# First-layer expert weights loaded in 16 transfers from ScalarE's DMA queue instead of 40 from SyncE's, with three reorderings in the attention steps

## The chip, the cores and the metric

One core of a Trainium2 chip. The metric is the device time of one launch in microseconds (us); the times below are medians over runs.

## What is computed

Three layers follow each other on 2 batches of 768 tokens with 8 heads of 40 (320 features). The first is a gated linear attention, written in the reference as a recurrence over time:

```python
m_new = np.maximum(f_gate[:, :, t] + m, i_gate[:, :, t])
f_stab = np.exp(f_gate[:, :, t] + m - m_new)
i_stab = np.exp(i_gate[:, :, t] - m_new)
C = f_stab[:, :, None, None] * C + i_stab[:, :, None, None] * np.einsum('bhd,bhe->bhde', vt, kt)
n = f_stab[:, :, None] * n + i_stab[:, :, None] * kt
h_tilde = np.einsum('bhde,bhe->bhd', C, qt)
nq = np.einsum('bhd,bhd->bh', n, qt)[:, :, None]
denom = np.maximum(np.abs(nq), 1.0)
y[:, :, t] = o * h_tilde / denom          # o = sigmoid(o_gate)
```

The second is a soft mixture of 8 experts with 4 slots each: `logits = x @ phi`, a softmax over tokens gathers 32 slot inputs, each expert does `relu(s @ w1[e]) @ w2[e]` (w1 is 320 x 1024, w2 1024 x 320), and a softmax over slots spreads the results to the tokens. The third is a mixture of 4 dense experts over all 1536 tokens with weights u1 and u2 of the same sizes. All data are 32-bit floats.

## The kernel before, in words

Every engine's instructions are written out by hand in one order (`tc.manual_schedule()`); the framework only adds the waits. Each DMA gets one of eight completion semaphores, dealt out in turn in the program's order over all issuing engines, and a DMA is issued only after the DMA before it on its semaphore has landed.

**Attention** goes over NT = 12 tiles of 128 tokens, i = 0 to 11, the two batches in turn. The loop `for i in range(2, NT - 1)` interleaves stages of several tiles: `stage_S(i)` multiplies q and k on TensorE, `stage_W` masks and scales on VectorE, `stage_E(i + 1)` makes the next tile's decay matrix (TensorE, then two exponentials on ScalarE), `stage_P1(i - 1)` multiplies with v, `stage_K(i + 2)` transposes k on TensorE (`stage_KT`, L313) and copies it out on ScalarE (`stage_KC`, L318), `q_pad`, `qT_mm` and `qT_copy` do so for q, `stage_B` takes the absolute value of the denominator on ScalarE (L394), which `stage_N` then uses on VectorE (L399), `stage_X` and `stage_XC` transpose a finished tile. The gates of tiles are made by `gates1a`, `gates1b`, `gates_hi` and `gates2`, for the last piece (chunks 4 and 5) in steps 3 to 6. All transposes and the decay matrices share three PSUM banks with the tag "t".

**Loads.** Everything comes through SyncE's queue (SP), in program order: per step one k tile (`load_k`, L198), one v tile (`load_v`, L205), one or two o_gate tiles (`load_o`, L220), in some steps q (`load_q`), each 160 KB in runs of 160 bytes, and between them w1 in 40 pieces of 256 KB (`load_w1`, L88: one of five rows per partition each). The table NW says how many pieces stand in each step; the last is issued after the attention. k, v and q rotate through few buffers, so their loads wait for the engines that read the buffer before.

**First mixture.** When the attention's memory is free, w2 is loaded in 16 transfers of 640 KB (`load_w2`, L96), while TensorE does logits, gather and the w1 products (L1119), then the w2 products (L1155). Behind w2 come u1 and u2 of the first dense expert.

**Second mixture.** From about 120 us TensorE runs without a break (L1268, L1284).

Of the kernel before, what the change touches and what calls it, by code (L numbers as in the profile page):

```python
# [8 lines left out]
F32 = mybir.dt.float32  # L9
# [5 lines left out]
NEG = -1.0e30  # L15
NBIG = 11
NW3 = 5
NW = (0, 0, 4, 4, 4, 4, 4, 4, 4, 4, 3, 2)
WN = (2, 4, 2, 4)


# [1 line left out]
def tile_mlstm_soft_moe_domain_moe(  # L23
# [57 lines left out]
    u1s = {}  # L81
    u2s = {}

    def load_w1(n, r):
        half, j = divmod(n, 4)
        if r == 0:
            w1s[half, j] = slot([128, 5, FH], f"w1_{n}")
        nc.sync.dma_start(  # L88
            out=w1s[half, j][:, r],
            in_=w1[2 * j:2 * j + 2, :, half * FH:half * FH + FH].rearrange("e (p r) f -> r (e p) f", r=5)[r],  # L90
        )

    def load_w2(e, u, get):
        if u == 0:
            w2s[e] = get([128, 2, R2, DM], f"w2_{e}")
        nc.sync.dma_start(out=w2s[e][:, u], in_=w2[e, u * FH:(u + 1) * FH].rearrange("(p r) d -> p r d", r=R2))  # L96
# [10 lines left out]
            u2s[e] = get([128, FT, DM], f"u2_{e}")  # L107
        nc.sync.dma_start(out=u2s[e][:, r0:r1], in_=u2[e, r0 * 128:r1 * 128].rearrange("(r p) d -> p r d", p=128))

    wq = [("a", n, r) for n in range(8) for r in range(5)] + [("b", e, u) for e in (0, 2, 4, 6) for u in range(2)]  # L110
    wq += [("b", e, u) for e0 in (1, 5) for u in range(2) for e in (e0, e0 + 2)]

    def load_w(n=1, get=None):
        for _ in range(n):
            if wq:
                kind, x, u = wq.pop(0)
                if kind == "a":
                    load_w1(x, u)
                else:
                    load_w2(x, u, get or slot)  # L120

    with tc.manual_schedule():
        mctx = ExitStack()
# [9 lines left out]
        with ExitStack() as actx:  # L133
# [258 lines left out]
            def stage_B(i):  # L392
                dn = wp.tile([128, H], F32, tag="dn", name="dn")
                nc.scalar.activation(out=dn, in_=hs[i][0][:, :, D], func=AF.Abs, scale=2.0)  # L394
                dns[i] = dn
# [56 lines left out]
                pXs[i] = pt  # L452

            def stage_XC(i):
                xT = tp.tile([128, 3, 128], F32, tag="xT", bufs=4, name="xT")
                nc.scalar.activation(out=xT, in_=pXs.pop(i)[:, 0:3], func=AF.Copy)
                xTs[i] = xT

# [19 lines left out]
                lts[i0] = (lt, et)  # L478
                return lambda: nc.scalar.activation(out=lt, in_=pl[:, 0:128], func=AF.Copy)

            def stage_M(i0, get=tt_):
                lt, et = lts.pop(i0)
                pl = get()
                nc.tensor.transpose(pl[:, 0:128], et, ident)
                dE = tp.tile([128, 128], F32, tag="dE", bufs=2, name="dE")
                nc.scalar.activation(out=dE, in_=pl[:, 0:128], func=AF.Copy)
                dEs[i0] = dE
                plg[i0] = pl
                ltk[i0] = lt

            plg = {}
            ltk = {}

            def copy_lg(i0):
                nc.tensor.transpose(plg[i0][:, 128:256], ltk.pop(i0), ident)
                nc.vector.tensor_copy(lg[:, i0:i0 + 4, :], plg.pop(i0)[:, 128:256].rearrange("p (j n) -> p j n", n=NS))

            def stage_Q(i0, get=tt_):
# [194 lines left out]
            def gates_hi(c0, c1):  # L693
                nc.scalar.activation(out=hiX[:, c0 * L:c1 * L].bitcast(F32R), in_=X[:, c0 * L:c1 * L], func=AF.Copy)
# [85 lines left out]
            stage_O(1)  # L780
            load_k(4)
            load_os()
            load_w(2)
            load_q(5)
            stage_Wk(2)
            stage_T2(1)
# [2 lines left out]
            for i in range(2, NT - 1):  # L789
                c = bc(i)[1]  # L790
                last = i == NT - 2
                stage_S(i)
                if i + 3 < NT:
                    load_k(i + 3)
                if i in (4, 5):
                    load_q(i + 2)
                load_w(1)
                load_os(2 if i in (5, 6) else 1)
                if i + 2 < NT:
                    load_v(i + 2)  # L800
                load_w(NW[i] - 1)
                if i == 3:
                    nc.sync.dma_start(out=phi_sb[:, 0:2, :], in_=phi[0:256].rearrange("(k p) n -> p k n", p=128))
                    nc.sync.dma_start(out=phi_sb[0:64, 2, :], in_=phi[256:320])
                stage_W(i, 0)
                stage_E(i + 1)
                stage_P2(i)
                if i in (3, 4, 7, 8):
                    q_pad({3: 4, 4: 5, 7: 6, 8: 7}[i], 0, 2, A_)
                stage_W(i, 1)  # L810
                if i == 2:
                    gates1b(2, 4, 0, 0)
                stage_U(i)
                stage_P1(i - 1)
                if i > 2:
                    stage_T2(i)
                stage_mask(i + 1)
                if i == 2:
                    stage_V(1)
                    stage_K(3)  # L820
                    stage_V1(1)
                    gates1b(2, 4, 0, 1)
                    stage_T2(i)
                    qT_mm(3, 0)
                    qT_copy(3, 0)
                    gates_hi(2, 4)
                    gates1b(2, 4, 1)
                    gates2(2, 4, (A_, V_, G_, G_, A_))
                if i == 6:
                    gates1b(4, NC, 1)  # L830
                stage_V(i)
                stage_T1(i - 1)
                stage_B(i - 1)
                if last:
                    break
                if i in (3, 6):
                    tokT(*((2, 4) if i == 3 else (4, NC)))
                    tokC(*((2, 4) if i == 3 else (4, NC)))
                if i == 6:
                    gates2(4, NC, (A_, V_))  # L840
                if i == 8:
                    stage_R0(stage_Q(0))
                if i == 9:
                    c_sum(0, 4)
                    emit_c4(0)
                if i == 7:
                    stage_M(0)
                    copy_lg(0)
# [24 lines left out]
                if i == 2:
                    pt = tr().rearrange("p a b -> p (a b)")
                    gate_rows(1, 4, NC, pt, 0)
                    gate_rows(0, 4, NC, pt, 2 * L)
                    gates_in(4, NC, pt[:, 0:2 * L], pt[:, 2 * L:4 * L])
                if i in (3, 4, 5):
                    gates1a(4, NC, Fg[:, 4 * L:S], (i - 3,))
                if i == 5:  # L880
                    gates1b(4, NC, 0, 0)
                    gates1b(4, NC, 0, 1)
                    gates_hi(4, NC)
                if i == 6:
                    gates2(4, NC, (None, None, G_, A_, G_))
# [124 lines left out]
        with mctx:  # L1010
# [54 lines left out]
            stage_M(8, tt_)  # L1065
# [313 lines left out]
```

## Time and profile before

| | |
|---|---|
| time, median of 3 runs | 322.2 us (321.8 to 323.55) |
| the profiled execution's own time | 323.63 us |
| its span | 321.5 us |
| TensorE busy | 304.8 us, 95% |
| VectorE, ScalarE, GpSimd busy | 168.9 us, 117.6 us, 93.2 us |
| DMA | 43.48 MB, 65518 packets, 49808 of them under 512 bytes |
| granted clock of TensorE | 1.00 (2.4 GHz) in every slice |

A profile belongs to one execution, here one that took 323.63 us; the span is what the profiler saw of it. Its first 80 us are the attention, about 80 to 120 us the first mixture, the rest the second one. Busy shares over the whole span hide the difference between these stages, so the views used here are cut by stage.

### The profile page before, as it was taken

The numbers are of one execution on the slowest core, as the hardware profiler recorded it, in microseconds if no ns is written. First come the engines' busy times: TensorE is split into PE (matmuls) and PEld (weight loads), VectorE is DVE, ScalarE is ACT, GpSimd is POOL, SyncE is SP. The second block draws the span as 40 slices with busy tenths as digits, with TensorE's granted clock in tenths as the row PEclk, the third lists the DMA queues.
The fourth block names the chain that finished last, engine by engine and source line by source line (L and its number), as shares of the span: only waits on it lengthen the run. The fifth ranks groups of instructions, "written<-read, shape, count | busy, mean of one in ns | idle before, by whom it ended". The sixth has DMA issues, their size and how long they took to land.

```text
span 321.5 us, 6949 instructions
## 1 busy us (share of the span) xinstructions
PE 304.8 (95%) x2846; PEld 266.5 (83%) x2846; DVE 168.9 (53%) x351; ACT 117.6 (37%) x259; POOL 93.2 (29%) x148
## 2 busy tenths in 40 slices
PE   8899988888899899999999999999999999999995
PEld 7787876667553348899999998999998999999995
DVE  7997997667434144564444444444443444444411
ACT  3968747553412034432222222333332222222200
POOL 8657766543602027830004600003800000000000
PEclk9999999999999999999999999999999999999999
DMA  7999979999999998129000001380001100011111
GB/s 139 195 232 215 231 205 251 217 243 296 341 417 416 387 308 200 26 59 314 0 3 0 0 2 33 78 283 2 0 0 27 42 2 0 22 41 41 43 61 41
DMA packets 65518, 43.48 MB, mean 135 GB/s; under 512 B 49808, under 2 KB 57008, under 8 KB 65488
## 3 DMA queue, kind: packets, MB, share of 16 engines
q1 hardware_dynamic: 65392, 42.99, 47.1%
q8 instruction: 22, 0.36, 0.5%
q14 instruction: 8, 0.07, 0.1%
q10 hardware_dynamic: 96, 0.07, 0.1%
HBM read 39.50 MB, written 1.97 MB: 129 GB/s over the span
## 4 chain that ended last, share of the span: by engine, by line
PE 81%; DVE 7%; DMA 6%; issue 1%; ACT 1%; SPq 1%; POOL 1%; ACTq 0%; DVEq 0%; POOLq 0%
PE po L1284 53%; PE pa L1268 7%; DMA w<-in_moe_w_dram 3%; DMA kvb<-in_k_dram 3%; PE pss L346 3%; PE po L1155 2%; PE pg L1224 2%; PE ph L1119 1%; PE p L370 1%; DVE w L352 1%; PE p L362 1%; PE pt L451 1%; PE pt L270 1%; PE pt L296 1%; PE p L544 1%
## 5 line engine op out<-in xcount | busy, mean ns | idle before, releaser
L1284 PE MATMUL po<-uh,hh 128*128 128x320 f32 x768 | 170.3, 309 | 0.6 <-ACT hh L1273 0.6
L1284 PEld LDWEIGHTS po<-uh,hh 128*128 128x128 f32 x768 | 131.7, 188 | 5.8 <-issue 1.8
L1284 PE MATMUL po<-ul,hh 128*128 128x320 f32 x384 | 118.2, 309 | 0.0
L1274 DVE SCALAR_TENSOR_TENSOR hh<-pa,hh 128x512 fp32r<-128x512 f32 x96 | 65.7, 691 | 95.5 <-ACT hh L1273 95.5
L1273 ACT ACTIVATE hh<-pa 128x512 fp32r<-128x512 f32 x96 | 56.7, 599 | 121.7 <-PE pa L1268 120.5
L1284 PEld LDWEIGHTS po<-ul,hh 128*128 128x128 f32 x384 | 72.0, 188 | 0.0
L1209 POOL TENSOR_SCALAR uh<-u 128x640 fp32r<-128x640 f32 x16 | 11.6, 728 | 93.2 <-PE po L1284 73.5
L1268 PE MATMUL pa<-cS,gs 128*128 128x512 f32 x96 | 36.9, 397 | 0.2 <-ACT gs L1262 0.2
L1211 POOL TENSOR_TENSOR ul<-u,uh 128x640 fp32r<-128x640 f32 x16 | 25.1, 1570 | 1.3
L1292 DVE SCALAR_TENSOR_TENSOR acc<-po,pr,acc 128x320 f32<-128x320 f32 x36 | 19.5, 543 | 10.6 <-PE po L1284 10.6
L1268 PEld LDWEIGHTS pa<-cS,gs 128*128 128x128 f32 x96 | 17.9, 188 | 1.2 <-issue 0.4
L352 DVE TENSOR_TENSOR w<-w,pss 128x512 f32<-128x512 f32 x24 | 15.3, 679 | 4.4 <-PE pss L346 3.4
L305 POOL TENSOR_SCALAR_AFFINE_SELECT w<-w 128x512 f32<-128x512 f32 x24 | 15.5, 668 | 6.9 <-ACT w L299 6.9
L346 PE MATMUL pss<-qT,kT 64*128 64x128 f32 x192 | 14.1, 286 | 0.0
L299 ACT ACTIVATE w<-pt 128x512 f32<-128x512 f32 x24 | 13.0, 596 | 2.4 <-PE pt L296 2.3
L346 PEld LDWEIGHTS pss<-qT,kT 64*128 64x128 f32 x192 | 11.8, 187 | 1.8 <-issue 0.7
L1155 PE MATMUL po<-w,hT 128*32 128x320 f32 x128 | 10.6, 434 | 1.3 <-DMA w<-in_moe_w_dram 1.3
L370 PE MATMUL p<-kvb,w 128*64 128x64 f32 x320 | 11.0, 222 | 0.0
L443 POOL TENSOR_TENSOR x<-x,rd 128x320 f32<-128x320 f32 x11 | 8.8, 801 | 7.0 <-DVE rd L400 7.0
L370 PEld LDWEIGHTS p<-kvb,w 128*64 128x64 f32 x320 | 10.3, 138 | 0.2 <-issue 0.2
L1155 PEld LDWEIGHTS po<-w,hT 128*32 128x32 f32 x128 | 4.2, 110 | 7.1 <-DMA w<-in_moe_w_dram 2.5
L313 PE MATMUL pt<-ident,kvb 128*128 128x128 f32 x40 | 6.4, 283 | 3.4 <-DMA kvb<-in_k_dram 3.3
(248 smaller groups left out, 310.5 us busy)
## 6 DMA issues: line engine op xcount, KB each, us to landing
w<-in_moe_w_dram SPq DMA_DIRECT2D x40, 256.0 KB, 4.5
w<-in_moe_w_dram SPq DMA_DIRECT2D x16, 640.0 KB, 11.4
u1a<-in_moe_w_dram SPq DMA_DIRECT2D x4, 1024.0 KB, 10.3
u<-in_moe_w_dram SPq DMA_DIRECT2D x3, 1280.0 KB, 10.1
kvb<-in_k_dram SPq DMA_DIRECT2D x12, 160.0 KB, 4.2
kvb<-in_v_dram SPq DMA_DIRECT2D x12, 160.0 KB, 4.3
x<-in_o_gate_dram SPq DMA_DIRECT2D x12, 160.0 KB, 4.6
out_dram<-acc SPq DMA_DIRECT2D x12, 160.0 KB, 1.8
```

The costliest lines, as they stand in the source:

```text
L299: nc.scalar.activation(out=w.rearrange("p g t -> p (g t)"), in_=pt, func=AF.Exp)
L305: nc.gpsimd.affine_select(out=w, in_=w, compare_op=ALU.is_ge, fill=0.0, base=0, pattern=[[0, HP], [1, L]], channel_multiplier=-1)
L346: nc.tensor.matmul(out=pss[j][:, g, :], lhsT=kT[i][64 * j:64 * j + 64, g, :], rhs=q_of(i)[64 * j:64 * j + 64, g, :], start=True, stop=True)
L352: nc.vector.tensor_tensor(out=w, in0=w, in1=pS.pop((i, j)), op=ALU.mult)
L370: nc.tensor.matmul(out=p1[64 * x:64 * x + 64, h, :], lhsT=W[i, h % 2][:, h // 2, 64 * x:64 * x + 64], rhs=vb(i)[:, h, :], start=True, stop ...
L1155: nc.tensor.matmul(out=pos[hf][32 * j:32 * j + 32, 0:DM], lhsT=hT[:, r, 32 * j:32 * j + 32], rhs=w2s[2 * j + hf][:, r // R2, r % R2, :], s ...
L1211: nc.gpsimd.tensor_tensor(out=lo[:, r0:r0 + 2], in0=raw[:, r0:r0 + 2], in1=hi[:, r0:r0 + 2].bitcast(F32), op=ALU.subtract)
L1268: nc.tensor.matmul(out=pa, lhsT=GS[e][0][:, ft * 128:(ft + 1) * 128], rhs=cS[:, tg * 512:(tg + 1) * 512], start=True, stop=True)
L1273: nc.scalar.activation(out=hi, in_=pa, func=AF.Relu)
L1274: nc.vector.scalar_tensor_tensor(out=lo, in0=pa, scalar=0.0, in1=hi.bitcast(F32), op0=ALU.max, op1=ALU.subtract)
L1284: nc.tensor.matmul(out=po[:, 0:DM], lhsT=x[:, sl], rhs=y[e][:, ft, :], start=(ft == 0 and n == 0), stop=(ft == FT - 1 and n == 2))
L1292: nc.vector.scalar_tensor_tensor(out=dst, in0=po[:, 0:DM], scalar=pr[:, i, e:e + 1], in1=dst, op0=ALU.mult, op1=ALU.add)
```

## The change

1. w1 is loaded by 16 transfers (two rows, then three rows, of each of 8 tiles: 512 and 768 KB) that ScalarE issues: one ahead of the loop, one in step 2 and two each in steps 3 to 9, behind the exponentials of `stage_E(i + 1)`. SyncE's queue keeps k, v, q, o_gate, phi, probs and, later, w2.
2. `stage_B(i - 1)` moves from before `stage_K(i + 2)` to after the q copies and `stage_X`, in ScalarE's order; in step 3 and in the tail it moves behind other copies.
3. The last gate piece: its first two accumulations are done one and two steps sooner, `gates1b(4, NC, 1)` in step 5 instead of 6, and `gates2` in one place, ahead of the transposes, with five engines named (A, V, G, A, G).
4. The xT tiles get five buffers instead of four, and `stage_M` transposes the logits together with their exponentials, except for the last group.

```diff
-NW = (0, 0, 4, 4, 4, 4, 4, 4, 4, 4, 3, 2)
+NW = (1, 1, 2, 2, 2, 2, 2, 2, 2, 0)
...
-    def load_w1(n, r):
+    def load_w1(n, r0, r1):
         half, j = divmod(n, 4)
-        if r == 0:
+        if r0 == 0:
             w1s[half, j] = slot([128, 5, FH], f"w1_{n}")
-        nc.sync.dma_start(
-            out=w1s[half, j][:, r],
-            in_=w1[2 * j:2 * j + 2, :, half * FH:half * FH + FH].rearrange("e (p r) f -> r (e p) f", r=5)[r],
+        nc.scalar.dma_start(
+            out=w1s[half, j][:, r0:r1],
+            in_=w1[2 * j:2 * j + 2, :, half * FH:half * FH + FH].rearrange("e (p r) f -> (e p) r f", r=5)[:, r0:r1],
         )
+
+    w1q = [(n, r0, r1) for n in range(8) for r0, r1 in ((0, 2), (2, 5))]
+
+    def act_w(k=1):
+        for _ in range(k):
+            if w1q:
+                load_w1(*w1q.pop(0))
...
             load_os()
-            load_w(2)
+            act_w(NW[0])
             load_q(5)
...
-                load_w(1)
                 load_os(2 if i in (5, 6) else 1)
                 if i + 2 < NT:
                     load_v(i + 2)
-                load_w(NW[i] - 1)
...
                 stage_E(i + 1)
+                act_w(NW[i - 1])
                 stage_P2(i)
...
                 if i == 6:
-                    gates1b(4, NC, 1)
+                    gates2(4, NC, (A_, V_, G_, A_, G_))
                 stage_V(i)
                 stage_T1(i - 1)
-                stage_B(i - 1)
...
                 if i > 2:
                     stage_X(i - 2)
+                if i != 3:
+                    stage_B(i - 1)
                 if i == 3:
                     stage_XC(1)
+                    stage_B(2)
...
-                if i in (3, 4, 5):
-                    gates1a(4, NC, Fg[:, 4 * L:S], (i - 3,))
+                if i == 3:
+                    gates1a(4, NC, Fg[:, 4 * L:S], (0,))
+                    gates1b(4, NC, 0, 0)
+                if i == 4:
+                    gates1a(4, NC, Fg[:, 4 * L:S], (1, 2))
                 if i == 5:
-                    gates1b(4, NC, 0, 0)
                     gates1b(4, NC, 0, 1)
                     gates_hi(4, NC)
+                    gates1b(4, NC, 1)
...
-            load_w(9, slot3)
+            load_w(8, slot3)
```

ScalarE's order in step 2, with the semaphores that each instruction waits for (w are the decay tiles of `stage_E(3)`, gt the result of `gates_hi`). Before:

```order
L394 ACTIVATE dn<-t_339 128x8 [waits DVE_49]
L327 ACTIVATE x_1_98<-x_1_98 128x320 [waits DMAHW7_49]
L299 ACTIVATE w<-pt 128x512 [waits PE_49] x2
L318 ACTIVATE kT<-pt 128x512 [waits PE_49]
L284 ACTIVATE qT<-pt 128x512 [waits PE_49]
L694 ACTIVATE gt_95<-gt_95 128x256 [waits DVE_49]
```

and now:

```order
L398 ACTIVATE dn<-t_339 128x8 [waits DVE_49]
L331 ACTIVATE x_1_98<-x_1_98 128x320 [waits DMAHW7_49]
L88 DMA w_0_379<-in_moe_w_dram 128x2x512 [waits DMAHW7_49]
L303 ACTIVATE w<-pt 128x512 [waits PE_49] x2
L88 DMA w_0_379<-in_moe_w_dram 128x3x512 [waits DMAHW0_49]
L322 ACTIVATE kT<-pt 128x512 [waits PE_49]
L288 ACTIVATE qT<-pt 128x512 [waits PE_49]
L702 ACTIVATE gt_95<-gt_95 128x256 [waits DVE_49]
```

Two DMA issues came between; the first waits for the o_gate load that holds DMAHW7 before it, the second for the v load on DMAHW0 (the last rows but one of the next block).

SyncE's queue around the same place (x_1 is an o_gate tile, kvb a k or v tile). Before:

```order
L220 DMA x_0_97<-in_o_gate_dram 128x8x40 [waits DMAHW4_49]
L88 DMA w_0_379<-in_moe_w_dram 128x512 [waits DMAHW5_49]
L88 DMA w_0_379<-in_moe_w_dram 128x512 [waits DMAHW6_49]
L193 DMA qb<-in_q_dram 128x8x80 [waits DMAHW7_49]
L198 DMA kvb_87<-in_k_dram 128x8x40 [waits DMAHW0_49]
L88 DMA w_0_379<-in_moe_w_dram 128x512 [waits DMAHW1_49]
L220 DMA x_1_98<-in_o_gate_dram 128x8x40 [waits DMAHW2_49]
```

and now:

```order
L224 DMA x_0_97<-in_o_gate_dram 128x8x40 [waits DMAHW4_49]
L197 DMA qb<-in_q_dram 128x8x80 [waits DMAHW5_49]
L202 DMA kvb_87<-in_k_dram 128x8x40 [waits DMAHW6_49]
L224 DMA x_1_98<-in_o_gate_dram 128x8x40 [waits DMAHW7_49]
L209 DMA kvb_87<-in_v_dram 128x8x40 [waits DMAHW0_49]
L202 DMA kvb_85<-in_k_dram 128x8x40 [waits DMAHW1_49,PE_49,Pool_49]
```

The three w1 pieces ahead of that o_gate load are gone, and no w1 piece stands between the later k, v and o_gate loads either.

ScalarE's order in step 4 (qx is `q_pad`, dn `stage_B`). Before:

```order
L299 ACTIVATE w<-pt 128x512 [waits PE_49] x2
L250 ACTIVATE qx<-qb 128x16x40 [waits DMAHW7_49]
L394 ACTIVATE dn<-t_577 128x8 [waits DVE_49]
L318 ACTIVATE kT<-pt 128x512 [waits PE_49]
L284 ACTIVATE qT<-pt 128x2x2x128 [waits PE_49] x2
```

and now:

```order
L303 ACTIVATE w<-pt 128x512 [waits PE_49] x2
L88 DMA w_2_664<-in_moe_w_dram 128x2x512 [waits DMAHW7_49]
L88 DMA w_2_664<-in_moe_w_dram 128x3x512 [waits DMAHW0_49]
L254 ACTIVATE qx<-qb 128x16x40 [waits DMAHW5_49]
L322 ACTIVATE kT<-pt 128x512 [waits PE_49]
L288 ACTIVATE qT<-pt 128x2x2x128 [waits PE_49] x2
L398 ACTIVATE dn<-t_571 128x8 [waits DVE_49]
```

The wait for VectorE went behind the k and q copies, and two DMA issues came ahead of them.

## Rows read from the trace of the kernel before

**Rows 1.** Busy time by stretch: start:end, length, busy us per engine, clock, DMA share, GB/s.

```profile
30.00:40.00 10.00, 10.00 (x167) 8.60 (x169) 8.10 (x20) 8.46 (x21) 6.19 (x10) 1.00 0.95 219
40.00:50.00 10.00, 8.68 (x165) 7.16 (x162) 9.64 (x21) 4.73 (x14) 7.47 (x11) 1.00 0.82 200
50.00:60.00 10.00, 8.75 (x163) 7.28 (x159) 6.11 (x16) 7.95 (x20) 4.80 (x8) 1.00 0.99 241
60.00:70.00 10.00, 7.21 (x130) 5.86 (x126) 6.98 (x19) 4.29 (x11) 5.35 (x9) 1.00 0.99 246
70.00:80.00 10.00, 9.28 (x198) 7.91 (x196) 7.03 (x19) 4.05 (x11) 3.75 (x7) 1.00 0.95 274
80.00:108.00 28.00, 25.25 (x242) 12.97 (x244) 11.21 (x35) 6.24 (x19) 7.39 (x20) 1.00 1.03 394
...
130.00:320.00 190.00, 188.06 (x1267) 180.02 (x1265) 84.44 (x140) 53.55 (x91) 27.29 (x24) 1.00 0.15 47
```

**Rows 2.** The chain that ended last, in order of time: start us, us, what.

```profile
50.88 4.02 DMA kvb<-in_k_dram
...
64.73 4.77 DMA kvb<-in_k_dram
...
97.20 10.61 DMA w<-in_moe_w_dram
```

**Rows 3.** Waits of TensorE, 20 to 80 us: total us, times, longest.

```profile
PE pt L313 <- DMA kvb<-in_k_dram: 3.3, 3, 1.4
PE pt L270 <- ACT gs L676: 0.8, 1, 0.8
PE pt L296 <- POOL x L443: 0.8, 1, 0.8
```

**Rows 4.** Waits of TensorE, 100 to 112 us.

```profile
PE po L1155 <- DMA w<-in_moe_w_dram: 1.3, 2, 0.9
```

**Rows 5.** ScalarE in order of time, step 2, idle before in brackets.

```profile
18.84 0.45 ACT L327 ACTIVATE x<-x 128x320 f32<-128x320 f32 x1
...
21.54 0.60 ACT L318 ACTIVATE kT<-pt 128x512 f32<-128x512 f32 x1 [1.14 <-PE pt L313]
...
22.51 0.42 ACT L694 ACTIVATE gt<-gt 128x256 fp32r<-128x256 f32 x1
```

**Rows 6.** SyncE's queue in order of time: start us, us, issue, out and source, count.

```profile
17.14 1.09 SPq L88 DMA_DIRECT2D w<-in_moe_w_dram  x2
...
19.39 1.74 SPq L88 DMA_DIRECT2D w<-in_moe_w_dram  x1
21.17 0.44 SPq L220 DMA_DIRECT2D x<-in_o_gate_dram  x1
...
73.66 4.07 SPq L88 DMA_DIRECT2D w<-in_moe_w_dram  x8
...
80.10 1.21 SPq L88 DMA_DIRECT2D w<-in_moe_w_dram  x1
81.42 17.27 SPq L96 DMA_DIRECT2D w<-in_moe_w_dram  x16
```

**Rows 7.** DMA issues of the page: count, KB each, median us from issue to landing.

```profile
w<-in_moe_w_dram SPq DMA_DIRECT2D x40, 256.0 KB, 4.5
...
x<-in_o_gate_dram SPq DMA_DIRECT2D x12, 160.0 KB, 4.6
```

**Rows 8.** How long one issue takes on SyncE (ns min/median/max), w1 and v loads.

```profile
L88 SPq DMA_DIRECT2D w<-in_moe_w_dram x40: 365/505/3043, 17.1 to 80.1; - x40
...
L205 SPq DMA_DIRECT2D kvb<-in_v_dram x12: 434/1121/1949, 5.9 to 73.2; - x12
```

**Rows 9.** VectorE in order of time, step 3.

```profile
31.79 0.19 DVE L684 TENSOR_TENSOR gs<-kv,gs 128x32 f32<-128x32 f32 x1 [1.72 <-PE kv L682]
```

**Rows 10.** Waits of ScalarE, 20 to 80 us.

```profile
ACT dn L394 <- DVE t L386: 7.0, 7, 1.5
ACT kT L318 <- PE pt L313: 6.7, 5, 2.4
```

More of the change, by code (lines that the diff above doesn't have):

```diff
@@ L108, in load_u2 @@
         nc.sync.dma_start(out=u2s[e][:, r0:r1], in_=u2[e, r0 * 128:r1 * 128].rearrange("(r p) d -> p r d", p=128))
-    wq = [("a", n, r) for n in range(8) for r in range(5)] + [("b", e, u) for e in (0, 2, 4, 6) for u in range(2)]
-    wq += [("b", e, u) for e0 in (1, 5) for u in range(2) for e in (e0, e0 + 2)]
+    wq = [(e, u) for e in (0, 2, 4, 6) for u in range(2)]
+    wq += [(e, u) for e0 in (1, 5) for u in range(2) for e in (e0, e0 + 2)]
     def load_w(n=1, get=None):
@@ L115, in load_w @@
             if wq:
[L116 to L120, printed above, removed]
+                e, u = wq.pop(0)
+                load_w2(e, u, get or slot)
     with tc.manual_schedule():
@@ L454, in stage_XC @@
             def stage_XC(i):
-                xT = tp.tile([128, 3, 128], F32, tag="xT", bufs=4, name="xT")
+                xT = tp.tile([128, 3, 128], F32, tag="xT", bufs=5, name="xT")
                 nc.scalar.activation(out=xT, in_=pXs.pop(i)[:, 0:3], func=AF.Copy)
@@ L479, in stage_L, with stage_M @@
                 return lambda: nc.scalar.activation(out=lt, in_=pl[:, 0:128], func=AF.Copy)
-            def stage_M(i0, get=tt_):
+            def stage_M(i0, get=tt_, both=True):
                 lt, et = lts.pop(i0)
@@ L484, in stage_M @@
                 nc.tensor.transpose(pl[:, 0:128], et, ident)
+                if both:
+                    nc.tensor.transpose(pl[:, 128:256], lt, ident)
                 dE = tp.tile([128, 128], F32, tag="dE", bufs=2, name="dE")
@@ L488, in stage_M @@
                 plg[i0] = pl
-                ltk[i0] = lt
+                if not both:
+                    ltk[i0] = lt
             plg = {}
@@ L494, in copy_lg @@
             def copy_lg(i0):
-                nc.tensor.transpose(plg[i0][:, 128:256], ltk.pop(i0), ident)
+                if i0 in ltk:
+                    nc.tensor.transpose(plg[i0][:, 128:256], ltk.pop(i0), ident)
                 nc.vector.tensor_copy(lg[:, i0:i0 + 4, :], plg.pop(i0)[:, 128:256].rearrange("p (j n) -> p j n", n=NS))
@@ L838, in tile_mlstm_soft_moe_domain_moe @@
                     tokC(*((2, 4) if i == 3 else (4, NC)))
-                if i == 6:
-                    gates2(4, NC, (A_, V_))
                 if i == 8:
@@ L877, in tile_mlstm_soft_moe_domain_moe @@
                     gates_in(4, NC, pt[:, 0:2 * L], pt[:, 2 * L:4 * L])
-                if i in (3, 4, 5):
-                    gates1a(4, NC, Fg[:, 4 * L:S], (i - 3,))
+                if i == 3:
[3 more added lines that the diff above has]
+                    gates1a(4, NC, Fg[:, 4 * L:S], (1, 2))
                 if i == 5:
-                    gates1b(4, NC, 0, 0)
                     gates1b(4, NC, 0, 1)
                     gates_hi(4, NC)
+                    gates1b(4, NC, 1)
                 if i == 6:
-                    gates2(4, NC, (None, None, G_, A_, G_))
                     tokM(4, NC)
@@ L928, in tile_mlstm_soft_moe_domain_moe @@
             stage_O(iL)
+            stage_B(iL - 2)
             stage_XC(iL - 3)
-            load_w(1)
             stage_S(iL)
-            load_w(NW[iL] - 1)
             stage_G(iL - 2)
@@ L1064, in tile_mlstm_soft_moe_domain_moe @@
             warm(WN[1])
-            stage_M(8, tt_)
+            stage_M(8, tt_, False)
             for j in range(4):
```

## The prediction

> **What bounds the kernel now.** I read the busy time by stretch first, since the change touches only the first 80 us and what starts behind them. From 130 to 320 us TensorE is busy 188.06 of 190 us and the DMA share is 0.15 [rows 1]: nothing here shortens that stage, it can only start sooner or later. From 30 to 80 us two things are nearly full at once: TensorE is busy 43.9 of 50 us, and the DMA share is 0.82 to 0.99. From 80 to 108 us the DMA share is 1.03. So the early part is short of DMA time as much as of TensorE time.
>
> The chain of waits, read next, says where the shortage bites. Twice a k load stands in it for four to five microseconds, and at 97.20 us a w2 transfer for 10.61 us [rows 2]. Then the waits of TensorE: between 20 and 80 us it stood 3.3 us, in three places, for k tiles that had not landed, 0.8 us behind ScalarE's gate copy and 0.8 us at `stage_E` behind GpSimd [rows 3]; in the w2 products it stood 1.3 us for w2 [rows 4]. The reader is to see that k is late because of where it stands: SyncE's queue has w1 pieces ahead of it, and the order shows four to a step.
>
> **The change, part by part.**
>
> *k, v and o_gate without w1 ahead of them.* With no w1 in SyncE's queue, a k load goes out when its buffer is free. By the order the k tile of step i + 3 needs only readers of tile i - 3, and one ScalarE step, `q_pad`, for a q load ahead of it; that is more than a step sooner than now. The three waits, 3.3 us, should go. Bounds: 0, if the loads are as late as now, and 3.3. I take 3.3, as k was at most 1.4 us late each time.
>
> *The last gate piece.* `gates2` ahead of GpSimd's other work of step 6 lets the 0.8 us wait at `stage_E` go [rows 3]; bounds 0 and 0.8, I take 0.8. The gate accumulations themselves are moved, not removed: VectorE does them in 30 to 40 us, where it is busy 8.10 of 10 us, instead of 40 to 50 us, where it is busy 9.64 [rows 1]. Cover is there but thin; I count 0, and if VectorE has no room left in step 3 the next term grows.
>
> *ScalarE's first transfer.* This is the place that can lose. ScalarE comes to it after the tanh, at 18.84 + 0.45 = 19.3 us [rows 5]. By the order it shares its semaphore with the o_gate load of step 2, and must wait until that has landed. That load went out at 21.17 us, behind three w1 pieces of 1.09 + 1.74 = 2.83 us together [rows 6]; without them at 18.3 us. With the median 4.6 us to landing [rows 7] it lands at 22.9 us. So ScalarE stands still for 3.6 us, with the exponentials of `stage_E(3)`, the k and q copies and `gates_hi` queued behind it, then spends two issues of 0.505 us each (median of w1's on SyncE [rows 8]), 4.6 us in all. The 1.14 us in which it waited for TensorE there anyway comes off [rows 5]: `gates_hi`, at 22.51 us now, is some 3.5 us late. VectorE waits for it at once, and has 1.72 us of idle time in step 3 to make up [rows 9]. So 1.8 us stay. Upper bound 3.5, with no idle time to use; lower bound 1.0, if the 0.8 us behind ScalarE's gate copy [rows 3] goes too, because `stage_B` no longer stands ahead of it. I take 1.8: the slack of VectorE is the nearest row.
>
> *ScalarE's other transfers.* Steps 3 to 9 add 14 issues: 14 x 0.505 = 7.1 us. Moving `stage_B` behind the copies takes away the 7.0 us in which ScalarE waited for VectorE with the k copy queued behind [rows 10]. The two cancel, 0 net. Bounds: 14 x 0.365 = 5.1 us and 14 x 1.121 = 15.7 us, the last if an issue is held up as the v loads are on SyncE [rows 8]. I stay with w1's own row, which is the same data.
>
> *xT buffers and `stage_M`.* A fifth buffer and a joint transpose take waits of a few tenths away; no row here is as large as the other terms, so 0, and up to 0.5 better.
>
> Attention: -3.3 - 0.8 + 1.8 = -2.3 us.
>
> *w2.* Its first transfer is issued at 81.42 us, when the attention's memory is free. By then w1 pieces of the last 4.5 us, the median to landing [rows 7], are still ahead: two of the eight issued from 73.66 us on (0.5 us apart, until 77.7 us) and the one of 80.10 us [rows 6]. Three pieces of 0.26 MB at 394 GB/s [rows 1] are 2.0 us. In the change all w1 is issued by step 9. What TensorE can take of this is its wait, 1.3 us [rows 4]. So the stage behind would start 2.3 + 1.3 = 3.6 us sooner.
>
> *The cap.* The same bytes must still pass the same DMA engines before the w2 products can end. What is to be had is what they leave unused: from 30 to 80 us the shares leave 0.05 + 0.18 + 0.01 + 0.01 + 0.05 of 10 us each, 3.0 us [rows 1]. This is less than 3.6, so I take **-3.0 us**. From about 120 us on everything moves with it.
>
> The sum is against the profiled execution, 323.63 us, and gives 320.6; that execution took 1.4 us more than the median of the runs, 322.2, from which I expect **319.2 us**.
>
> **The rivals.** What a measurement of this kernel can tell from no change is about 0.5%, 1.6 us.
>
> *DMA work only changes places.* w1 now runs beside the small loads instead of between them, more of it per step: two transfers of 1.28 MB together instead of four pieces of 1.02 MB. The shares of 0.95 to 0.99 leave little room [rows 1], so k may land as late as now although issued sooner. Then 3.3 us stay, the first transfer still costs 1.8, the gates give 0.8 and w2 1.3: -0.3 us, **321.9 us**. For it speaks the 1.03 behind 80 us; against it the 0.82 from 40 to 50 us, just ahead of two of the late k tiles, and that w1 is not needed before the attention has ended. The Trainium skill (DMA: Bandwidth & Descriptors, section "Issuing engines are not separate DMA queues") says that DMAs of all issuing engines run on the same 16 engines, and that a second issuer saves only the issue time, which is usually small; by that rule this rival is the likely one. The same page (section "Queues, rings and completion order") has each DMA engine take turns between the queues it has work for; by that a k tile would no longer wait for all of the w1 ahead of it, which speaks for my forecast. No row here shows two loaded queues at once.
>
> *ScalarE becomes the bound: slower.* If each of the 14 issues takes 1.121 us, as the v loads do on SyncE [rows 8], ScalarE loses 15.7 + 3.5 = 19.2 us. It has 7.0 us from `stage_B` and 6.7 us in which its k copies waited for TensorE [rows 10], of which the 3.3 us for late k go. That leaves 8.8 us on k and q copies that `stage_S` needs, against 0.8 + 3.3 + 1.3 = 5.4 us of gain: +3.4 us, **325.6 us**. It decides from (5.4 + 10.4 - 3.5) / 14 = 0.88 us an issue. For it speaks the maximum of 3.0 us among w1's issues; against it that the median is 0.505 and that ScalarE's own queue carries no small runs.
>
> *ScalarE does not stand still.* If the o_gate load lands before ScalarE comes to its first transfer, the 1.8 us fall away and the 0.8 us behind the gate copy is gained: 3.3 + 0.8 + 0.8 + 1.3 = 6.2 us; the cap at the share of 1.03 seen behind 80 us is 3.0 + 0.03 x 50 = 4.5 us: **317.7 us**. Against it the 3.6 us of distance.
>
> **How the numbers follow.** Forecast 0.44 (of it 0.41 faster, 0.03 same), DMA work changes places 0.23 (0.21 same, 0.02 faster), ScalarE bound 0.18 (0.16 slower, 0.02 same), no standstill 0.15 (faster). Faster 0.58, same 0.26, slower 0.16. The range goes from 317.0 us, the best case and 0.7 us for the small terms at their better ends, to 323.0 us, the second case with the first transfer at nearly its upper bound (1.8 to 3.0 us); what it leaves out is nearly all of the ScalarE case.
>
> **What would show it.** Right: no wait of TensorE for k in the waits; ScalarE idle for 3 to 4 us at its first L88 issue, released by a DMA, and VectorE waiting there; w2's first issue near 79 us with no w1 landing behind it; the DMA share from 40 to 50 us near 0.95 or more. Wrong: TensorE still waiting for k (DMA work), w1 issues on ScalarE around 1 us with the k and q copies behind them (ScalarE bound), or the exponentials of step 2 at 19.3 us as now. The forecast falls as a whole if w2's first issue is not sooner than 81 us.

## The result and the profile after

The change makes the kernel slower: 326.05 us median of 20 runs (322.69 to 330.31), against 321.81 (319.09 to 324.52) for the kernel before on the same chip. The ratio is 1.0106, 95% interval 1.008 to 1.0133; it leaves out runs over 1.5% above the fastest of their kernel, eight of these 20, and is for that reason below the ratio of the medians. The forecast was 319.2 us, with 0.16 on slower, and its range ended at 323.0.

The profiled execution took 323.16 us, with a span of 321.1. It is one of the better runs: the spans go from 320.6 to 328.2 us, and the mean granted clock falls as they grow, from 0.983 to 0.968 or 0.969. So the profile shows the loss near its smallest: its span is even 0.4 us shorter than that of the profiled execution before (321.5), which at 323.63 us was one of its kernel's longer ones. What is read from it below is where the gain was lost; the size of the loss comes from the 20 runs.

Busy time by stretch after the change, columns as in [rows 1] (length, TensorE, its weight loads, VectorE, ScalarE, GpSimd, granted clock, DMA share, GB/s):

```profile
30.00:40.00 10.00, 10.00 (x149) 8.66 (x145) 9.21 (x23) 8.53 (x24) 7.98 (x13) 1.00 1.01 312
40.00:50.00 10.00, 8.61 (x185) 7.22 (x183) 9.29 (x22) 4.03 (x9) 8.15 (x13) 1.00 1.04 262
50.00:60.00 10.00, 5.33 (x47) 4.63 (x49) 2.26 (x7) 4.91 (x16) 0.73 (x2) 0.54 1.09 254
60.00:70.00 10.00, 10.00 (x168) 8.54 (x164) 6.33 (x16) 6.34 (x14) 5.94 (x9) 0.95 1.04 279
70.00:80.00 10.00, 10.00 (x191) 8.59 (x191) 8.91 (x24) 6.50 (x18) 6.18 (x10) 1.00 0.49 168
...
130.00:320.00 190.00, 187.66 (x1264) 179.81 (x1260) 84.17 (x139) 53.55 (x91) 24.27 (x21) 1.00 0.15 47
```

The stage behind 130 us is as it was. The 20 us before 50 us are better fed than before (312 and 262 GB/s against 219 and 200 in [rows 1]). Then one stretch of 10 us breaks down: all four compute engines fall, and TensorE, half idle, is granted 0.54 of full speed, that is mostly the lower of its two levels, 1.2 GHz. From 70 to 80 us the DMA engines, at 0.95 before, are half empty.

Waits from 20 to 80 us: TensorE's two, ScalarE's two for loads, VectorE's longest:

```profile
PE pt L455 <- issue: 6.1, 1, 6.1
PE pt L274 <- ACT w L303: 0.8, 1, 0.8
...
ACT EL L666 <- DMA x<-in_o_gate_dram: 6.2, 1, 6.2
...
ACT qx L254 <- DMA kvb<-in_k_dram: 1.5, 1, 1.5
...
DVE dn L403 <- ACT dn L398: 6.5, 3, 5.3
```

The k waits of [rows 3] are gone, and one stop of 6 us has come. Its place, from the engines' rows in order of time, of ScalarE (first stretch and stop), TensorE and VectorE:

```profile
20.12 0.46 ACT L331 ACTIVATE x<-x 128x320 f32<-128x320 f32 x1
22.43 0.46 ACTq L88 DMA_DIRECT2D w<-in_moe_w_dram  x1
...
46.05 1.08 ACT L303 ACTIVATE w<-pt 128x512 f32<-128x512 f32 x2
51.12 2.15 ACTq L88 DMA_DIRECT2D w<-in_moe_w_dram  x2
53.31 0.60 ACT L666 ACTIVATE EL<-gt,gs 128x256 fp32r<-128x256 f32 x1 [6.18 <-DMA x<-in_o_gate_dram]
...
47.95 0.66 PE L317 MATMUL pt<-ident,kvb 128*128 128x128 f32 x4
54.67 0.87 PE L455 MATMUL pt<-ident,x 128*128 128x128 f32 x3 [6.06 <-issue]
...
49.58 0.71 DVE L441 SCALAR_TENSOR_TENSOR x<-x,t 128x320 f32<-128x320 f32 x1
55.62 0.17 DVE L403 TENSOR_SCALAR dn<-dn 128x8 f32<-128x8 f32 x1 [5.33 <-ACT dn L398]
```

ScalarE ends its exponentials at 47.1 us and stands until the first of two w1 issues goes out at 51.12; the second goes out late too, and L666 starts at 53.31, released by an o_gate load. But L666 reads gt and gs, and no o_gate tile. What waited for that load is the w1 issue ahead of it in ScalarE's order: every SyncE or ScalarE transfer takes one of the eight completion semaphores in turn, and goes out only when the transfer that had it last has landed. By the program's order the first piece of step 6 follows a k load of SyncE, the second an o_gate load. The k tile is for a step three later. The rows of these loads, the k load of 44.10 us and the two o_gate loads of 48.5 and 49.7 us, give the time from issue to landing:

```profile
44.10 4.37 SPq L202 DMA_DIRECT2D kvb<-in_k_dram  x1
...
DMA to landing us min/median/max: 6.9/6.9/6.9
...
DMA to landing us min/median/max: 3.1/3.4/3.7
```

The k load landed at 44.10 + 6.9 = 51.0 us, and the first w1 issue went out at 51.12; the second o_gate load landed at 49.7 + 3.1 = 52.8 us, and the second w1 issue went out at 52.9. SyncE itself was behind: the issue of that k load alone took 4.37 us, the longest of the twelve.

So one late prefetch stopped ScalarE, and a second load held it a little longer. With ScalarE stood the denominators (VectorE), the copies out of the "t" banks and the transposes that need those banks (TensorE). For TensorE this is read from the order: the row of L455 names no releaser, but it starts at 54.67 us, 0.1 us after ScalarE's copies out of "t" tiles that start at 54.31 and 54.39 us and take 0.18 us each.

ScalarE's own issues are short, and the small loads land no sooner than before (k 4.2, v 4.3, o_gate 4.6 us there). First the issue in ns (min/median/max), then issues of the page with the median us to landing, as in [rows 7]:

```profile
L88 ACTq DMA_DIRECT2D w<-in_moe_w_dram x16: 374/375/885, 22.4 to 72.5; - x16
```

```profile
w<-in_moe_w_dram ACTq DMA_DIRECT2D x8, 768.0 KB, 6.5
w<-in_moe_w_dram ACTq DMA_DIRECT2D x8, 512.0 KB, 4.5
...
kvb<-in_k_dram SPq DMA_DIRECT2D x12, 160.0 KB, 4.5
kvb<-in_v_dram SPq DMA_DIRECT2D x12, 160.0 KB, 5.3
x<-in_o_gate_dram SPq DMA_DIRECT2D x12, 160.0 KB, 4.9
```

### The profile page after: what moved, and what is told of

Same layout as the page of the kernel before. It is cut to its first block, busy times and chain, and to the rows that moved or that the text cites. A ratio compares the mean times of both kernels' runs of the same rounds, so it can differ in the third digit from the quotient of the medians.

```text
span 321.1 us, 6916 instructions
## 1 busy us (share of the span) xinstructions
PE 307.5 (96%) x2846; PEld 271.3 (84%) x2846; DVE 167.2 (52%) x351; ACT 117.8 (37%) x259; POOL 92.6 (29%) x148
## 4 chain that ended last, share of the span: by engine, by line
PE 72%; DVE 1%; ACT 1%; issue 0%; POOL 0%; ACTq 0%
PE po L1292 53%; PE pa L1276 7%; PE ph L1127 3%; PE po L1163 3%; PE pg L1232 2%; PE kvp L990 1%; PE s L997 1%; PE pt L1035 1%; PE pt L1120 0%; PE pt L1090 0%; PE pt L1176 0%; DVE x L441 0%; PE po L1263 0%; PE pt L455 0%; POOL x L447 0%
## 5 line engine op out<-in xcount | busy, mean ns | idle before, releaser
L309 POOL TENSOR_SCALAR_AFFINE_SELECT w<-w 128x512 f32<-128x512 f32 x24 | 14.8, 641 | 6.4 <-ACT w L303 6.4
L350 PE MATMUL pss<-qT,kT 64*128 64x128 f32 x192 | 15.0, 299 | 0.0
L350 PEld LDWEIGHTS pss<-qT,kT 64*128 64x128 f32 x192 | 12.6, 198 | 1.8 <-issue 0.6
L455 PE MATMUL pt<-ident,x 128*128 128x128 f32 x36 | 6.5, 295 | 6.7 <-issue 6.1
L374 PE MATMUL p<-kvb,w 128*64 128x64 f32 x320 | 11.7, 230 | 0.0
L374 PEld LDWEIGHTS p<-kvb,w 128*64 128x64 f32 x320 | 11.0, 146 | 0.2 <-issue 0.2
L455 PEld LDWEIGHTS pt<-ident,x 128*128 128x128 f32 x36 | 4.1, 147 | 8.0 <-issue 6.6
L1163 PE MATMUL po<-w,hT 128*32 128x320 f32 x128 | 9.2, 434 | 0.0
```

The lines of the kernel that those rows point to most:

```text
L309: nc.gpsimd.affine_select(out=w, in_=w, compare_op=ALU.is_ge, fill=0.0, base=0, pattern=[[0, HP], [1, L]], channel_multiplier=-1)
L350: nc.tensor.matmul(out=pss[j][:, g, :], lhsT=kT[i][64 * j:64 * j + 64, g, :], rhs=q_of(i)[64 * j:64 * j + 64, g, :], start=True, stop=True)
L374: nc.tensor.matmul(out=p1[64 * x:64 * x + 64, h, :], lhsT=W[i, h % 2][:, h // 2, 64 * x:64 * x + 64], rhs=vb(i)[:, h, :], start=True, stop ...
L1163: nc.tensor.matmul(out=pos[hf][32 * j:32 * j + 32, 0:DM], lhsT=hT[:, r, 32 * j:32 * j + 32], rhs=w2s[2 * j + hf][:, r // R2, r % R2, :], s ...
```

## The theories

- **A, the tie.** ScalarE's w1 issues wait, through shared semaphores, for SyncE's loads; where such a load is late, ScalarE and all behind it stop, and TensorE drops to the lower clock.
- **B, two loaded queues.** w1 beside the small loads makes k, v and o_gate late; the hold of ScalarE is a side effect.
- **C, the orders.** The reordered steps cost, not the loads.
- **D, DMA time,** against **E, TensorE and its partners**: whether transfers or the engines set the end up to about 115 us.

All ratios below are to the kernel before, run beside each group on the same chip.

## Taking the change apart

**The orders alone.** The w1 loads go back to SyncE, in 40 pieces, at their old places:

```diff
-NW = (1, 1, 2, 2, 2, 2, 2, 2, 2, 0)
+NW = (0, 0, 4, 4, 4, 4, 4, 4, 4, 4, 3, 2)
...
-                act_w(NW[i - 1])
+                load_w(1)
...
+                load_w(NW[i] - 1)
```

> The three reorderings alone: the w1 pieces go back to SyncE, in 40 transfers at the places of the kernel before. Theory A (ScalarE stands at its w1 issues until a late SyncE load has landed, and TensorE's clock falls behind that stop): no instruction of ScalarE waits on a w1 issue, the granted clock is 1.00 from 30 to 100 us, the tanh and denominator waits go as forecast, and the time is 0.985 to 0.995 of before (317 to 320 us). Theory B (w1 and the small loads contend, whoever issues): the k waits of before (3.3 + 3 us) stay, time 0.990 to 1.003. Theory C (the new orders are what costs): 1.008 to 1.015, 324 to 327 us, with new waits at the denominators or the last gate piece.

Measured: 1.0046 (1.0014 to 1.0077), 321.35 us. No theory had this: A wanted a gain, C a loss of twice the size and more. The interval reaches into B's range, which ends at 1.003, but the k waits that B wanted to stay fell to 1.1 us. The profiled run (319.91 us) has shorter k waits than [rows 3], but a longer w2 wait than [rows 4]:

```profile
PE po L1162 <- DMA w<-in_moe_w_dram: 2.3, 2, 2.0
PE pt L313 <- DMA kvb<-in_k_dram: 1.1, 2, 0.7
```

and the stretch from 100 to 110 us lost clock (0.83):

```profile
100.00:110.00 10.00, 7.99 (x79) 2.99 (x79) 0.29 (x1) 0.33 (x1) 0.00 (x0) 0.83 1.04 341
```

The attention ended sooner (w2's first issue at 75.87 us, 81.42 in [rows 6]), and TensorE came to w2 ahead of its loads. Among this kernel's runs the one at a mean clock of 1.000 took 319.12 us, one at 0.989 323.11.

**w1 alone.** The other half: 16 transfers from ScalarE in the kernel before, old orders (the w1 lines of the change and nothing else).

> The w1 part alone: 16 transfers from ScalarE, the orders of the attention steps as before. Theory A: slower than before, 1.008 to 1.025 (324 to 330 us), ScalarE again held at a w1 issue for 3 to 6 us and TensorE at the lower clock for some 10 us after it. Theory B: the same or slower, 1.00 to 1.015, with late k, v or o loads that hold TensorE or VectorE directly. Theory C: no slower than before, 0.985 to 1.00.

Measured: 1.0165 (1.0125 to 1.0205), 325.05 us, as A had it. The same stop stands at the same place; this time the instruction behind the issue is the absolute value of a denominator, which reads t and is again released by an o_gate load:

```profile
51.05 2.18 ACTq L88 DMA_DIRECT2D w<-in_moe_w_dram  x2
53.28 0.22 ACT L398 ACTIVATE dn<-t 128x8 f32<-128x8 f32 x1 [4.20 <-DMA x<-in_o_gate_dram]
```

**One word.** The 16 transfers stay where they are and SyncE issues them:

```diff
-        nc.scalar.dma_start(
+        nc.sync.dma_start(
             out=w1s[half, j][:, r0:r1],
```

> The changed kernel with one word changed: the 16 w1 transfers are issued by SyncE, at the same places of the program, so sizes, steps and orders stay and only the issuing queue differs. Theory A: ScalarE is never held at a w1 issue, clock 1.00 from 30 to 100 us, 0.985 to 0.997 of before (317 to 321 us). Theory B: the bytes meet the same small loads, so it stays at 1.005 to 1.015 (323 to 327 us) with the same half-clock stretch near 50 us. Theory C: also 1.005 to 1.015, but with full clock.

Measured: 0.9998 (0.9968 to 1.0028), 319.58 us: just above A's range, below B and C. ScalarE is not held at a w1 issue, but k waits again, longer than before, and the clock that A wanted at 1.00 was 0.97 from 30 to 80 us:

```profile
PE pt L317 <- DMA kvb<-in_k_dram: 5.8, 3, 2.6
```

So ScalarE's queue did remove the k waits, as forecast, and cost more than it removed: 1.0106 against 0.9998.

**Other pairs.** In the changed kernel `act_w` moves ahead of the step's loads, which pairs each issue with another load:

```diff
+                act_w(NW[i - 1])
                 if i + 3 < NT:
                     load_k(i + 3)
...
-                act_w(NW[i - 1])
```

> The changed kernel with each step's w1 issues put ahead of the step's k, q, o and v loads and of the step's exponentials (still from ScalarE), so each issue is tied to another, older load of SyncE. Theory A: the hold of 5.3 us before the exponentials of step 7 becomes shorter or goes to another step; time 0.99 to 1.006 (319 to 324 us), below the changed kernel's 326. Theory B: the bytes come a little earlier beside the same loads: 1.005 to 1.02 (323 to 328 us). Theory C: 1.008 to 1.015, as the changed kernel.

Measured: 1.025 (1.019 to 1.031), 328.93 us, outside A's range and above B's, whose end its interval touches. (The hold of 5.3 us that the text before the run names is VectorE's, at the denominators; ScalarE's was 6.18 us, behind the exponentials of step 6.) The mechanism is A's all the same: the holds moved to other steps and there are three. In each an exponential, which reads only pt, is released by a load:

```profile
24.96 1.09 ACT L303 ACTIVATE w<-pt 128x512 f32<-128x512 f32 x2 [5.07 <-DMA kvb<-in_v_dram]
...
55.57 1.09 ACT L303 ACTIVATE w<-pt 128x512 f32<-128x512 f32 x2 [3.10 <-DMA kvb<-in_k_dram]
...
66.13 1.08 ACT L303 ACTIVATE w<-pt 128x512 f32<-128x512 f32 x2 [4.62 <-DMA kvb<-in_v_dram]
```

**Half as many transfers,** from ScalarE and from SyncE (the second with `nc.sync` as above):

```diff
-NW = (1, 1, 2, 2, 2, 2, 2, 2, 2, 0)
+NW = (0, 1, 1, 1, 1, 1, 1, 1, 1, 0)
...
-    w1q = [(n, r0, r1) for n in range(8) for r0, r1 in ((0, 2), (2, 5))]
+    w1q = [(n, r0, r1) for n in range(8) for r0, r1 in ((0, 5),)]
```

> The changed kernel with the two pieces of each w1 tile merged into one transfer: 8 of 1.31 MB from ScalarE, one in each of steps 2 to 9, so each step's bytes and the queue stay; only the number of transfers halves, and with it which SyncE load each issue is tied to: one that is issued about two steps earlier, not one. Theory A (the tie holds ScalarE): the long hold near 51 us goes, clock 1.00 from 40 to 70 us, time 0.99 to 1.003 of before (317 to 321 us). Theory B (a second loaded queue slows the small loads, the tie is a side effect): 1.006 to 1.015, with TensorE or VectorE waiting for k, v or o directly.

> The same 8 transfers of 1.31 MB in steps 2 to 9, issued by SyncE. Both theories: no hold of ScalarE at a w1 issue, k waits of 4 to 7 us in all as with 16 from SyncE; time 0.99 to 1.005. Theory A expects the 8 from ScalarE to be no slower than this; theory B expects them slower by 2 us or more.

Measured: 1.0142 (1.0081 to 1.0202) from ScalarE, 325.5 us, and 1.0014 (0.9976 to 1.0053) from SyncE, 319.75 us, with k waits of 6.4 us as expected. The first is a miss for A's number: I took it that a load of two steps ago has landed. It had not, and one of the eight issues still held ScalarE for 5.3 us:

```profile
60.12 0.55 ACTq L88 DMA_DIRECT2D w<-in_moe_w_dram  x1
60.72 0.74 ACT L254 ACTIVATE qx<-qb 128x640 f32<-128x640 f32 x1 [5.27 <-DMA kvb<-in_v_dram]
```

By ratios alone B was still open here: whenever ScalarE had the bytes it was slower, whenever SyncE had them it was not.

## How much the loads bind

Two kernels without the loads of the four odd w1 tiles, 5.2 MB: the kernel before, and the orders alone.

```diff
         half, j = divmod(n, 4)
+        if n % 2:
+            w1s[half, j] = w1s[half, j - 1]
+            return
```

> The kernel before, without the loads of the four odd w1 tiles (their matmuls read the tile before them): 20 of 40 transfers and 5.2 MB left out, which at the 417 GB/s of 90 to 100 us are 12.6 us of transfer. Theory D (up to 115 us the DMA engines set the end): faster by 3 to 8 us, 0.975 to 0.99 of before (312 to 317 us), the k waits and the w2 wait gone. Theory E (TensorE and its partners set the end, transfers hide): within 2 us of before, 0.994 to 1.0.

> The three reorderings with w1 as in the kernel before, and again without the loads of the four odd w1 tiles (5.2 MB left out). Theory D: with the transfers out of the way the orders give what was forecast of them, 2 to 3.5 us below the kernel before with the same loads left out, 0.965 to 0.98 of before (309 to 314 us). Theory C (the orders themselves cost): equal to it or 1 to 2 us above it.

Measured: 0.9915 (0.9885 to 0.9945), 317.8 us, and 0.9789 (0.975 to 0.9828), 313.42 us. The same orders that cost 1.4 us with all of w1 (321.35 against the 319.99 us of the kernel before beside them) gain 317.8 - 313.42 = 4.4 us with half of it. C falls. The kernel before gains 2.5 us from the omission (320.27 to 317.8), below D's 3 to 8 and beyond E's 2: part of the transfers hid behind other work. With the new orders they hide no longer, 321.35 - 313.42 = 7.9 us between two groups of runs. In neither run does TensorE wait for k or w2 any more. So with the new orders more of the transfer time stands in the end time than with the old ones, 7.9 against 2.5 us for the same bytes. One stretch of each shows it, columns as above:

```profile
60.00:70.00 10.00, 9.27 (x169) 7.76 (x167) 8.10 (x21) 6.73 (x17) 5.78 (x9) 1.00 0.95 251
```

for the orders alone, and without half of w1:

```profile
60.00:70.00 10.00, 10.00 (x193) 8.68 (x194) 9.00 (x24) 6.41 (x17) 6.27 (x10) 1.00 0.40 101
```

The changed kernel with the same omission:

> The changed kernel without the loads of the four odd w1 tiles (5.2 MB left out, 8 of ScalarE's 16 transfers; their matmuls read the tile before). Compare with the same omission where SyncE issues the w1 pieces (0.979 of before, 313.4 us). Theory A with late loads as its condition: with the DMA engines less full SyncE's loads are on time, the waits at ScalarE's issues are short, 0.975 to 0.985 (312 to 315.5 us). Theory A without that condition (each issue costs whatever the load): 0.985 to 0.995 (315.5 to 319 us).

Measured: 0.983 (0.9774 to 0.9886), 314.77 us. Its profile has no hold over 1.3 us behind a w1 issue, and its interval overlaps that of the orders with SyncE's loads. The tie cost little where loads were on time (v landed after 3.7 us, median, against 5.3). This rests on few runs: one of the five took 320.53 us.

## The tie by itself

**A tie without bytes.** All w1 from SyncE, and beside each of the 16 transfers one of 64 bytes from ScalarE:

```diff
+                nc.scalar.dma_start(out=tiny[:, x - 1:x], in_=phi[0:16, 0:1])
```

> All 16 w1 transfers from SyncE, as in the run with 16 from SyncE (0.9998 of before), and beside each one a transfer of 64 bytes that ScalarE issues at the same place and nobody reads. ScalarE's queue then carries next to no bytes, but each of its 16 issues waits, as in the changed kernel, for a completion semaphore that a SyncE load used last. Theory A (that wait is what costs): holds of ScalarE of 2 to 6 us right behind such issues, 1.005 to 1.02 of before (322 to 327 us). Theory B (the bytes of a second queue are what costs): 0.997 to 1.004 (319 to 321.5 us), no holds.

Measured: 0.9989 (0.9959 to 1.002), 320.42 us. A miss for A. ScalarE does wait behind these issues (by the order the two ahead of the row below follow an o_gate and a v load), but 2.3 us at the most:

```profile
31.13 0.74 ACT L257 ACTIVATE qx<-qb 128x640 f32<-128x640 f32 x1 [2.30 <-DMA tiny<-in_moe_phi_dram]
```

**Bytes without a tie.** GpSimd issues the 16 transfers of the changed kernel. By the program's order its transfers take eight semaphores of their own; the eight that the section on the kernel before gives to all engines are those of SyncE and ScalarE:

```diff
-        nc.scalar.dma_start(
+        nc.gpsimd.dma_start(
             out=w1s[half, j][:, r0:r1],
```

> The changed kernel with the 16 w1 transfers issued by GpSimd in ScalarE's place: the bytes still come from a second queue, but its transfers have completion semaphores of their own, so neither engine waits there for the other's loads. Theory A: ScalarE is never held at a w1 issue; the time is 0.985 to 1.003 of before, unless GpSimd's own issues delay its products (16 of some 1 us beside its 4 to 8 us busy in 10). Theory B: k, v and o are as late as in the changed kernel, TensorE or VectorE wait for them directly, 1.006 to 1.015.

Measured: 0.9933 (0.9906 to 0.9961), 318.33 us: faster than both kernels. B falls, and not for lack of late loads. They land later than in the changed kernel, v after 7.2 us against 5.3, o_gate after 6.2 against 4.9, k after 4.8 against 4.5:

```profile
kvb<-in_k_dram SPq DMA_DIRECT2D x12, 160.0 KB, 4.8
kvb<-in_v_dram SPq DMA_DIRECT2D x12, 160.0 KB, 7.2
x<-in_o_gate_dram SPq DMA_DIRECT2D x12, 160.0 KB, 6.2
```

Hardly anything waits for them: in the profiled run TensorE waits 0.8 us for k in all, the clock is 1.00 in every 10 us up to 130 us, and w2's first issue stands at 74.84 us (81.42 in [rows 6], 79.61 in the changed kernel, the last row here).

```profile
PE pt L317 <- DMA kvb<-in_k_dram: 0.8, 1, 0.8
...
74.84 21.45 SPq L103 DMA_DIRECT2D w<-in_moe_w_dram  x16
...
79.61 21.21 SPq L103 DMA_DIRECT2D w<-in_moe_w_dram  x16
```

GpSimd pays for its issues with busy time, some 0.77 us each:

```profile
L88 POOL DMA_DIRECT2D w<-in_moe_w_dram x16: 762/766/963, 20.0 to 67.8; - x16
```

**Both.** That kernel, with ScalarE's 64-byte transfers added as above, 1 KB in all:

> The w1 transfers from GpSimd, as in the run that took 0.9933 of before, and beside each a transfer of 64 bytes from ScalarE that nobody reads. The bulk is then in a queue of its own, and ScalarE's issues take completion semaphores after nearly the same SyncE loads as in the changed kernel (the second one of step 6 after the same k load). Theory A (the tie to a late load costs, once the bulk in a second queue has made that load late): ScalarE stands for 3 to 6 us behind such an issue, near 50 us, and most of the gain is lost: 0.998 to 1.012 of before (319.5 to 324 us). Theory B (ScalarE's bulk transfers cost through something else than the tie): no hold, 0.990 to 0.997 (317 to 319 us).

Measured: 1.0316 (1.0252 to 1.038), 330.02 us, 11.7 us more than the 318.33 without them (on another chip; the ratios, 1.0316 against 0.9933, are each to the kernel before beside it): A, and beyond its price. Two long holds, both on loads that the released instruction does not read:

```profile
52.78 0.32 ACTq L101 DMA_DIRECT2D tiny<-in_moe_phi_dram  x1
53.15 0.60 ACT L669 ACTIVATE EL<-gt,gs 128x256 fp32r<-128x256 f32 x1 [2.98 <-DMA kvb<-in_k_dram]
...
65.72 0.32 ACTq L101 DMA_DIRECT2D tiny<-in_moe_phi_dram  x1
66.08 0.74 ACT L257 ACTIVATE qx<-qb 128x640 f32<-128x640 f32 x1 [6.87 <-DMA kvb<-in_v_dram]
```

By its row the k load of 46.23 us landed after 6.5 us, at 52.7, and the v load of 57.29 us after 8.4 us, at 65.7: each issue goes out within 0.1 us of the landing of the load that has its semaphore. The clock there:

```profile
50.00:60.00 10.00, 6.69 (x83) 5.55 (x74) 5.68 (x15) 5.08 (x17) 7.10 (x11) 0.74 1.02 254
60.00:70.00 10.00, 5.78 (x60) 5.16 (x57) 2.18 (x7) 3.15 (x8) 2.17 (x4) 0.67 0.85 198
```

w2's first issue comes at 86.22 us, 11.4 us later than without. The added transfers move 1 KB beside 43 MB, and the small loads land no later with them (medians: k 3.8, v 5.1, o_gate 5.7 us), so it is not their bytes. Shown: holds of ScalarE at issues that are tied to late loads cost this much, and the changed kernel has such a hold. Needed for it are the tie and, in these runs, w1 in a second queue: with w1 in SyncE's own queue the same 16 small transfers cost nothing. Why the tie is harmless there was not settled. SyncE's w1 transfers take semaphores as well, so the pairs are other ones (by the order eight of the 16 small transfers follow a k, q, v or o_gate load there, 11 of ScalarE's 16 in the changed kernel), and its loads then come in one queue; no run separates the two.

## Why the prediction was wrong

- *k, v and o_gate without w1 ahead: right for the waits.* TensorE's k waits went, and came back at 5.8 us as soon as SyncE issued the 16 transfers. The loads were no faster for it, and one k load that nobody needed yet landed 6.9 us after its issue began.
- *The last gate piece: right.* The 0.8 us wait of TensorE behind GpSimd at the decay matrix is not among the waits after.
- *ScalarE's first transfer: mechanism right, size too large.* The o_gate load went out at 18.59 us (18.3 in the forecast) and landed after 3.8 us, not 4.6, and ScalarE came at 20.58 us, not 19.3. So it stood until 22.43 us, 1.85 and not 3.6 us, and TensorE waited 0.8 us for it, not the 1.8 I counted.
- *ScalarE's other transfers: the step that failed.* I counted their issue time, 14 x 0.505 us, set it against 7.0 us of removed waiting and put the sum at 0. The issue time was even less (median 0.375 us), and the denominator waits went nearly as expected (7.0 us before, 0.6 from 20 to 80 us after, and one of 2.4 us at 81.75 us). What I left out was the wait ahead of each issue. For the first transfer I had followed the shared semaphore to the load of SyncE that held it; for the 14 others I did not, though it is the same rule. Two of them together held ScalarE for 6.2 us in the profiled run, another for 1.5 us. The term's upper bound of 15.7 us spread the holding up evenly over 14 issues; it came as one long stop that the engines behind ScalarE could not hide.
- *The clock: not in the sum.* TensorE stood 6.1 us and then worked at the lower level (rows as in [rows 1]):

```profile
50.00:52.00 2.00, 0.00 (x0) 0.00 (x0) 0.29 (x1) 0.00 (x0) 0.00 (x0) 0.71 0.97 164
52.00:60.00 8.00, 5.33 (x47) 4.63 (x49) 1.97 (x6) 4.91 (x16) 0.73 (x2) 0.50 1.12 276
60.00:62.00 2.00, 2.00 (x48) 1.95 (x45) 0.88 (x2) 0.74 (x1) 2.00 (x4) 0.73 0.91 267
```

  It worked 5.33 us at 0.50 and 2.00 us at 0.73; at full clock the same work is 5.33 x 0.50 + 2.00 x 0.27 = 3.2 us shorter, an estimate from these rows. The mean of 0.983 over 321.1 us stands for (1 - 0.983) x 321.1 / 0.5 = 10.9 us at half speed, standing time included; that of 0.969 over 328.2 us for 20 us. That the longer runs had longer or more holds is inferred from this; only one run has a profile.
- *Attention and w2: right in kind, the hour by luck.* w2's first issue was forecast near 79 us and came at 79.61, and the w2 wait went. In the GpSimd kernel, without the stop, it comes at 74.84: the attention had more to gain than I counted, and the stop took most of that back. The prediction's own sign, w2's first issue ahead of 81 us, held in the profiled run and did not tell of the loss.
- *The cap: too simple.* I read 3.0 us of room from the shares of 30 to 80 us. The GpSimd kernel moved 281 GB/s there at a share of 0.99, where the kernel before moved 236 at 0.94. It issued w2 6.6 us sooner and ended only 2.1 us sooner (0.9933 x 320.06 = 317.9): from 80 to 118 us the DMA share is 1.04 before and 1.03 there. The orders alone, with w2's first issue 5.5 us sooner, gained nothing.

Of the rivals, *ScalarE becomes the bound* named 325.6 us, near the 326.05 measured, and the right engine, but by issues of 1.121 us, which ran at 0.375; its number was met by luck. *DMA work only changes places* held for SyncE's queue, where 16 transfers gave 0.9998. For a second queue with semaphores of its own it did not: 0.9933. The Trainium skill (DMA: Bandwidth & Descriptors, "Issuing engines are not separate DMA queues") says that a second issuer saves only the issue time. The runs do not contradict this: between SyncE's 16 and GpSimd's 16 lie 0.7%, SyncE's 16 issues took 0.581 us each (median), and whether the gain is that issue time or the small loads no longer standing behind w1, no run separates. But here a second issuer also cost more than it saved, 1.0106 from ScalarE, and the measurement decides.

## What to carry to other kernels

A transfer on a compute engine's queue is an instruction of that engine that waits for something: before you move one there, follow its semaphore to the transfer that held it last, for every issue and not for the first alone. When an instruction is released by a load that it does not read, look at the issue just ahead of it. Prefetches may land late at no cost, until a wait that has nothing to do with the data makes them due; a queue whose semaphores are its own (here GpSimd's) kept them harmless, and gave the fastest kernel of this study, 318.33 us.

## What the runs showed of the hardware

- Beside a loaded second queue the v loads (160 KB) landed later: 4.3 us (median) with all w1 in SyncE's queue in 16 transfers, 5.3 beside ScalarE's, 7.2 beside GpSimd's. Not all small loads did: k took 4.7, 4.5 and 4.8 us, o_gate 5.9, 4.9 and 6.2. The sum moved from 30 to 80 us was 281 GB/s in the GpSimd kernel, 236 in the kernel before.
- SyncE's single issues of a 160 KB load took up to 4.4 us in the changed kernel where ScalarE's of 512 and 768 KB took at most 0.885 us.
- GpSimd's issue of 512 or 768 KB took 0.77 us of GpSimd's busy time, and its transfers landed after 6.3 us (median).
- TensorE's granted clock fell while it stood (0.71 from 50 to 52 us) and stayed at the lower level through the work after 54.67 us: 0.50 until 60 us, 0.73 to 62 us, 1.00 again from 62 to 64 us. So the stop of 6.1 us was paid for a second time, by the estimate above with some 3.2 us.
